# Both attn @ v of a step between the scores of its two pairs of heads, and the ffn's first products ahead of the last attn @ v

## The chip, the cores and the metric

The kernel runs on one core of one Trainium2 chip. The core has a matrix engine (TensorE, PE in the rows; PEld is its weight load), VectorE (DVE), ScalarE (ACT), GpSimd (POOL) and SyncE (SP), which here issues all DMAs. Each engine takes its own instructions in the order in which they were written and waits on semaphores for the others. The metric is the device time of one execution in microseconds (us); lower is better.

## The reference

```python
def _attn_ref(q, k, v):                       # q, k, v: (8, 12, 448, 64), f32
    S = q.shape[2]
    scale = 1.0 / np.sqrt(q.shape[-1])
    scores = scale * np.matmul(q, k.transpose(0, 1, 3, 2)) - np.log(S)
    attn = 1.0 / (1.0 + np.exp(-scores))      # a sigmoid, not a softmax
    return np.matmul(attn, v)

def _moe_ref(x, w_in, w_out, s, b):           # x: (3584, 768), w_in: (768, 2048), w_out: (2048, 768)
    r = np.maximum(x @ w_in, 0.0)
    return (s * (r * r) + b) @ w_out

# x is the attention's output with its heads side by side, one row for each of 8 * 448 tokens
```

Attention has 8 batches of 12 heads, 448 tokens, 64 elements for a head; the feed-forward net (ffn) has 3584 tokens, a width of 768 and 2048 hidden units. Outputs are f32.

## The kernel before, in words

**Attention.** The work is cut in 24 quads, one for each batch and each group of four heads (two pairs i = 0, 1). A loop of 25 steps n treats quad n's scores and, one step behind, quad n-1's product with v, so that the sigmoid has a whole step to be done. In the words of this document, a step on TensorE consists of these groups:

- S0 and S1 (`scores`, L233): the scores of pair 0 and pair 1 against the first 384 keys, three PSUM tiles `psc` for each. Two heads share the array, 64 rows each: the records show the form 64*128. Each `psc` goes to ScalarE for a sigmoid (L224), which leaves an SBUF tile `a`.
- A0 and A1 (`attn_v`, L255): `a` times v of the step before, for pair 0 and pair 1, into the PSUM tiles `pav0` and `pav1`; form 128*64.
- SL (`scores_last`, L245): the scores against the last 64 keys for all four heads, one more `psc`; form 64*64. AL (`attn_v_last`, L264): the last 64 keys' part of the step before; form 64*64. After AL, `store_x` (L272) copies both `pav` to SBUF on VectorE and stores them.

Two matmuls in two halves of the array run side by side; of the f32 matmuls here the profile has two records each. The pool `ps_qk` has three `psc` of two banks, `ps_av` has one `pav0` and one `pav1`: all 8 banks. A `psc` is free again when its sigmoid is done, a `pav` when `store_x` has copied it.

**Weights beside it.** During attention the ffn's weights are decoded from 64-bit words, in 32 pieces (16 of w_out, 16 of w_in), on VectorE and ScalarE. A plan puts the parts of a piece on ticks; `tick()` is called twice in each step and issues what the plan holds for that tick. A piece with tick t is fetched by a DMA at t - 3 (`st`, L302); at t comes a VectorE operation (L122) and a ScalarE one (L125, which needs L122); at t + 1 two VectorE operations (L127, which needs L125, and L130); at t + 2 two more (L134, L137). Pieces follow each other by STEP ticks from FIRST on. For each pair of w_out pieces come "sums": four subtractions on VectorE at one tick, two casts on ScalarE (L155, which need the subtractions) at the next, two subtractions and two stores at the third. `st` and the sums' tiles share a pool of six buffers, `cx`. All of it stands in the engines' queues where the tick is called, between the sigmoids on ScalarE and between the copies of `store_x` on VectorE.

**From attention to the ffn.** The first block of 512 tokens is loaded back (`first_tokens`, L188), cast on ScalarE into its high part `x0h` (L341), and its rest `x0l` is made on VectorE (L106). `base(0, f)` makes the high part (L165, ScalarE) and the low part (L106, VectorE) of a block of w_in, `w_0_f`. `ffn1(f)` (L454) is a row of 18 matmuls into a PSUM tile `ph`: the first needs `x0h` and the high part of the weights, the second `x0l`, the third the low part of the weights. After attention, a loop over 16 blocks f runs `ffn1`, `activate` and the second product `ffn2` (L476, into `po`). The other six blocks of tokens are done in three pairs by a scheme that saves matmuls (L593, L659); the diff doesn't touch that.

The program is written out in Python in the order in which each engine will do it (`manual_schedule`); nothing reorders it later.

Of the kernel before, what the change touches and what calls it, by code (L numbers as in the profile page):

```python
# [10 lines left out]
F32 = mybir.dt.float32  # L11
# [7 lines left out]
PSUM = bass.MemoryType.PSUM  # L19
# [18 lines left out]
TB = 512  # L38
WARM = 4
PARTS = ((0, 0), (0, 1), (1, 0))  # L40
# [5 lines left out]
def sigmoid_attention_relu2_ffn(  # L46
# [11 lines left out]
    nc = tc.nc  # L58
    B, NQ, P, _, S = q.shape
    D = v.shape[5]  # L60
    NF, _, DM = w_in.shape
    NCC = DM // P
    HC = NCC // 2
# [9 lines left out]
    def pool(stack, name, bufs, side=None, space=None):  # L73
        kw = dict(side=side) if side else {}
        if space is not None:
            kw["space"] = space
        return stack.enter_context(
            tc.tile_pool(name=name, bufs=bufs, reuse_waits="tile", **kw)
        )
# [19 lines left out]
    def f32(ap):  # L99
        return ap.bitcast(F32)  # L100
# [8 lines left out]
    order = [f + h * NP for f in range(NP) for h in range(2)]  # L109
# [85 lines left out]
    at = ExitStack()  # L195
# [2 lines left out]
    ldv = pool(at, "ldv", 3)  # L198
    qk = ExitStack()
    ld = pool(qk, "ld", 2)  # L200
    ps_qk = pool(at, "ps_qk", 3, space=PSUM)
    ps_av = pool(at, "ps_av", 1, space=PSUM)

    half = (slice(0, D), slice(D, P))
    quads = [(b, t) for b in range(B) for t in range(NQ)]
    NL = len(quads)
# [33 lines left out]
    def scores_last(b, t, ld_):  # L240
        qt, kt, _ = ld_
        psc = ps_qk.tile([P, 2, 512], F32, tag="psc", name=f"psc_{b}_{t}_l")
        for j, r in enumerate(half):
            for i in range(2):
                nc.tensor.matmul(  # L245
                    psc[half[i], j, :S], kt[r, i, 3 * P :], qt[r, i, :],
                    start=True, stop=True,
                )
        return sigmoid(psc, f"{b}_{t}_l")

    def attn_v(b, t, i, ld_, a):
        pav = ps_av.tile([P, 512], F32, tag=f"pav{i}", name=f"pav_{b}_{t}_{i}")
        for c in range(3):
            for j, r in enumerate(half):
                nc.tensor.matmul(  # L255
                    pav[r, :S], ld_[2][:, 3 * i + c, j, :], a[c][:, j, :],
                    start=c == 0, stop=False,
                )
        return pav

    def attn_v_last(ld_, a, pavs):
        for i in range(2):
            for j, r in enumerate(half):
                nc.tensor.matmul(  # L264
                    pavs[i][r, :S], ld_[2][half[i], 6, j, :], a[half[i], j, :],
                    start=False, stop=True,
                )

    def store_x(b, t, pavs):
        for i in range(2):  # L270
            o = xo.tile([P, S], F32, tag="xo", name=f"xo_{b}_{t}_{i}")
            nc.vector.tensor_copy(o, pavs[i][:, :S])  # L272
            nc.sync.dma_start(x_dram[b][:, 2 * t + i], o)

    loaded = {0: load(*quads[0], first=True)}
# [8 lines left out]
    nc.sync.dma_start(b_sb, b_)  # L284


    FIRST, FETCH, STEP = 3, 3, 1.3

# [36 lines left out]
    def tick():  # L327
        for fn in plan.pop(next(ticks), ()):
            fn()

    x0 = []

    def first_tokens():
        for h in range(2):
            hi = cx.tile([P, HC, TB], F32R, tag="cx", name=f"x0h_{h}")
            lo = cx.tile([P, HC, TB], F32R, tag="cx", name=f"x0l_{h}")
            load_tokens(f32(lo), 0, h)
            x0.append((hi, lo))
        yield
        for hi, lo in x0:  # L340
            nc.scalar.copy(hi, f32(lo))  # L341
        yield
        for hi, lo in x0:
            sub(lo, f32(lo), f32(hi))

    prev = None
    for n in range(NL + 1):
        cur = quads[n] if n < NL else None
        a, pavs = [], []
        if n > 0 and n + 1 < NL:  # L350
            loaded[n + 1] = load(*quads[n + 1])
        if cur:
            a.append(scores(*cur, 0, loaded[n]))
        tick()
        if prev:
            pavs.append(attn_v(*quads[n - 1], 0, loaded[n - 1], prev[0]))
        if cur:
            a.append(scores(*cur, 1, loaded[n]))
        tick()
        if prev:  # L360
            pavs.append(attn_v(*quads[n - 1], 1, loaded[n - 1], prev[1]))
        if cur:
            a.append(scores_last(*cur, loaded[n]))
        if n == NL - 1:
            qk.close()
            p1 = pool(early, "p1", 2, side="right")
            ft = first_tokens()
            next(ft)
        if n == NL:
            next(ft)  # L370
            next(ft, None)
            w1 = base(0, 0)
            ts = sums(0, 0)
            next(ts)
        if prev:
            attn_v_last(loaded[n - 1], prev[2], pavs)
            store_x(*quads[n - 1], pavs)
        prev = a
    assert not plan
    at.close()  # L380
# [56 lines left out]


    raw_a = pool(ctx, "raw_a", 1)
    blk = ExitStack()  # L440
    p2 = pool(blk, "p2", 3)
    gp = pool(blk, "gp", 3)
    rt = pool(blk, "rt", 2)
    ot = pool(blk, "ot", 1)
    ps_h = pool(blk, "ps_h", 2, space=PSUM)
    ps_o = pool(blk, "ps_o", 1, space=PSUM)

    def ffn1(f, w):
        ph = ps_h.tile([P, TB], F32, tag="ph", name=f"ph_{f}")
        m = 0  # L450
        for c in range(NCC):
            h, cc = divmod(c, HC)
            for wi, xi in PARTS:
                nc.tensor.matmul(  # L454
                    ph, w[:, h, wi, cc * P : (cc + 1) * P], x0[h][xi][:, cc, :],
                    start=m == 0, stop=m == 3 * NCC - 1,
                )
                m += 1
        return ph

    def activate(f, ph):
        g = gp.tile([P, 2, TB], F32R, tag="g", name=f"g_{f}")
# [19 lines left out]
    held = None  # L482
    w2 = {}
    for i, f in enumerate(order):
        ph = ffn1(f, w1)
        if i + 1 < NF:
            w1 = base(0, order[i + 1])
        if i % 2 == 0:
            next(ts)
        g = activate(f, ph)  # L490
        for n in (i, i + 1):
            if n < NF and n not in w2:
                w2[n] = base(1, order[n])
        if held:
            ffn2(*held, i == 1, False)
        held = (w2[i], g)
        if i % 2 == 0:
            next(ts)
        elif i + 1 < NF:
            ts = sums(0, (i + 1) // 2)  # L500
            next(ts)
        if i == NF - 4:
            load_raw(0, 0)
        if i == NF - 2:
            early.close()
            roll = pool(ctx, "roll", AHEAD + 2, side="right")
            raw_b = pool(ctx, "raw_b", 1, side="right")
            gpool = pool(ctx, "gpool", 1, side="right")
            for _ in range(AHEAD):
                fetch()  # L510
            load_raw(0, 1)
# [41 lines left out]
    for n, (t1, t2) in enumerate(pairs):  # L553
# [31 lines left out]
        for u, (i, f) in enumerate(L1):  # L585
# [4 lines left out]
            m = 0  # L590
            for c in range(HC):
                for wi, xi in PARTS:
                    nc.tensor.matmul(  # L593
                        bk, wt[:, wi, c * P : (c + 1) * P], opd[i][xi][:, c, :],
                        start=i in (1, 6, 5) and m == 0,
                        stop=m == 3 * HC - 1,
# [54 lines left out]
        for j, (i, f) in enumerate(L2):  # L651
# [5 lines left out]
            for e in range(HC):  # L657
                for m, (wi, gi) in enumerate(PARTS):
                    nc.tensor.matmul(  # L659
                        bk[e], wt[:, wi, e * P : (e + 1) * P], g[:, gi, :],  # L660
                        start=i in (1, 4, 7, 5) and f == 0 and m == 0,
                        stop=f == NP - 1 and m == 2,
# [64 lines left out]
```

## Time and profile before

| | us |
|---|---|
| median of 3 runs | 1104.01 (1103.75 to 1104.33) |
| the profiled execution's own time | 1103.69 |
| its span, from the first to the last instruction | 1101.9 |
| TensorE busy in that span | 1092.8 (99%) |
| VectorE, ScalarE busy | 667.3, 519.5 |
| attention on TensorE (from 4.5 to 279.5 us of the span) | 275.0 |
| the first block of tokens in the ffn (279.5 to about 437) | 157.5 |
| the other six blocks | 665 |

The profile is of one execution. "Busy" is an average over stages with different limits, and a matmul's end is modelled. What is read for this change is the chain of waits in time, which gives each group on TensorE its length from the end of the group before to its own end, and the timeline of VectorE and ScalarE beside it.

### The profile page before, as it was taken

The page shows a single profiled execution, that of the slowest core. Times are in us where ns is not written, and L with a number is a line of the kernel's source. Part 1 is how long each engine was busy: PE and PEld are TensorE (multiplying, and loading weights), DVE is VectorE, ACT ScalarE, POOL GpSimd, SP SyncE. Part 2 cuts the span into 40 slices and gives each one's busy share as a digit, 9 for nine tenths or more (in the row PEclk, how much of TensorE's full clock was granted, in tenths as well). Part 3 has the DMA queues.
Part 4 walks back from the last instruction along what each step waited for, and adds up shares of the span by engine and source line. Part 5 has one row for each costly group of instructions (what it writes and reads, how often), then busy time and mean ns, then how long its engine had stood idle before and what let it go on. Part 6 is the DMA issues. An engine that isn't in the chain of part 4 may idle for free.

```text
span 1101.9 us, 13945 instructions
## 1 busy us (share of the span) xinstructions
PE 1092.8 (99%) x5140; PEld 777.0 (71%) x5140; DVE 667.3 (61%) x916; ACT 519.5 (47%) x681; POOL 0.2 (0%) x4
## 2 busy tenths in 40 slices
PE   8999999999999999999999999999999999999998
PEld 3333333333788887888888888888888888888887
DVE  2667777773866654646665654467564645574646
ACT  6777767776544444314543343135443351244341
POOL 0000000000000000000000000000000000000000
PEclk9999999999999999999999999999999999999999
DMA  7889899976576598668667586696676766666773
GB/s 287 303 286 337 322 331 323 330 286 210 223 286 259 220 353 316 194 200 303 191 182 233 172 301 196 192 309 193 195 220 196 275 196 192 196 190 196 220 195 130
DMA packets 99394, 268.30 MB, mean 244 GB/s; under 512 B 11776, under 2 KB 27648, under 8 KB 99328
## 3 DMA queue, kind: packets, MB, share of 16 engines
q1 hardware_dynamic: 99328, 267.43, 73.2%
q8 instruction: 41, 0.67, 0.3%
q14 instruction: 25, 0.20, 0.1%
HBM read 201.33 MB, written 66.06 MB: 243 GB/s over the span
## 4 chain that ended last, share of the span: by engine, by line
PE 95%; DMA 1%; DVE 1%; ACT 1%; SPq 0%; issue 0%; ACTq 0%
PE o L659 31%; PE h L593 29%; PE psc L233 11%; PE pav L255 10%; PE ph L454 6%; PE po L476 5%; PE psc_l L245 2%; PE pav L264 2%; DMA wu<-wb 1%; DMA out_t<-o 1%; SPq L394 0%; DVE s_l L106 0%; ACT s_h L412 0%; DVE G L542 0%; DVE p L103 0%
## 5 line engine op out<-in xcount | busy, mean ns | idle before, releaser
L659 PE MATMUL o<-gc,wu 128*128 128x512 f32 x1512 | 343.2, 389 | 0.0
L659 PEld LDWEIGHTS o<-gc,wu 128*128 128x128 f32 x1512 | 283.8, 188 | 58.9
L593 PE MATMUL h<-s_h,wu 128*128 128x512 f32 x1008 | 311.4, 389 | 2.0 <-ACT G L608 2.0
L593 PEld LDWEIGHTS h<-s_h,wu 128*128 128x128 f32 x1008 | 189.2, 188 | 42.1 <-ACT G L608 2.8
L593 PE MATMUL h<-s_l,wu 128*128 128x512 f32 x504 | 196.1, 389 | 0.0
L574 ACT CAST gc<-G 128x512 fp32r<-128x512 f32 x168 | 104.0, 621 | 188.9 <-PE o L659 157.4
L106 DVE TENSOR_TENSOR gc<-G,gc 128x512 fp32r<-128x512 f32 x168 | 115.3, 690 | 122.7 <-ACT gc L574 122.3
L545 ACT ACTIVATE G<-G,b_sb,s_sb 128x512 f32<-128x512 f32 x96 | 78.3, 816 | 175.6 <-DVE G L542 175.6
L224 ACT ACTIVATE a<-psc,nls 128x896 f32<-128x896 f32 x144 | 134.6, 1008 | 47.1 <-PE psc L233 47.1
L103 DVE TENSOR_TENSOR G<-G,h 128x512 f32<-128x512 f32 x120 | 82.4, 686 | 87.7 <-PE h L593 87.6
L233 PE MATMUL psc<-q,k 64*128 64x448 f32 x576 | 122.0, 557 | 0.0
L255 PE MATMUL pav<-a,v 128*64 128x448 f32 x576 | 118.6, 547 | 0.7 <-DVE xo L272 0.7
L593 PEld LDWEIGHTS h<-s_l,wu 128*128 128x128 f32 x504 | 94.6, 188 | 19.6
L233 PEld LDWEIGHTS psc<-q,k 64*128 64x128 f32 x576 | 51.7, 187 | 69.6 <-issue 47.3
L542 DVE SCALAR_TENSOR_TENSOR G<-G 128x512 f32<-128x512 f32 x96 | 66.4, 691 | 51.1 <-ACT G L610 48.6
L255 PEld LDWEIGHTS pav<-a,v 128*64 128x64 f32 x576 | 37.2, 136 | 76.5 <-issue 61.1
L272 DVE COPY xo<-pav 128x448 f32<-128x448 f32 x48 | 27.7, 619 | 74.8 <-PE pav L264 74.8
L476 PE MATMUL po<-g,w 128*128 128x512 f32 x288 | 67.7, 389 | 0.0
L476 PEld LDWEIGHTS po<-g,w 128*128 128x128 f32 x288 | 54.1, 188 | 11.2
L454 PE MATMUL ph<-x0h,w 128*128 128x512 f32 x192 | 61.7, 390 | 0.0
L106 DVE TENSOR_TENSOR G<-G,G 128x512 f32<-128x512 f32 x72 | 49.3, 685 | 0.0
L412 ACT CAST s_h<-raw 128x1536 fp32r<-128x1536 f32 x21 | 30.9, 1477 | 24.3 <-DVE raw L106 12.7
(55 smaller groups left out, 692.6 us busy)
## 6 DMA issues: line engine op xcount, KB each, us to landing
wu<-wt SPq DMA_DIRECT2D x192, 384.0 KB, 3.5
wu<-wb SPq DMA_DIRECT2D x144, 384.0 KB, 3.5
wt<-t SPq DMA_DIRECT2D x32, 768.0 KB, 5.2
wb<-w SPq DMA_DIRECT2D x48, 384.0 KB, 2.9
st<-w_out SPq DMA_DIRECT2D x16, 768.0 KB, 8.2
st<-w_in SPq DMA_DIRECT2D x16, 768.0 KB, 7.3
v<-v_t SPq DMA_DIRECT2D x24, 448.0 KB, 6.4
xd<-xo SPq DMA_DIRECT2D x48, 224.0 KB, 2.1
```

The source lines that it names most:

```text
L103: nc.vector.tensor_tensor(o, x, y, op=ALU.add)
L106: nc.vector.tensor_tensor(o, x, y, op=ALU.subtract)
L224: nc.scalar.activation(a, psc[:, :, :S], AF.Sigmoid, bias=nls, scale=SCALE)
L233: nc.tensor.matmul(psc[:, j, :S], kt[r, i, c * P : (c + 1) * P], qt[r, i, :], start=True, stop=True,)
L255: nc.tensor.matmul(pav[r, :S], ld_[2][:, 3 * i + c, j, :], a[c][:, j, :], start=c == 0, stop=False,)
L454: nc.tensor.matmul(ph, w[:, h, wi, cc * P : (cc + 1) * P], x0[h][xi][:, cc, :], start=m == 0, stop=m == 3 * NCC - 1,)
L476: nc.tensor.matmul(pos[e], w[:, h, wi, ee * P : (ee + 1) * P], g[:, gi, :], start=first and i == 0, stop=last and i == 2,)
L542: nc.vector.scalar_tensor_tensor(x, x, 0.0, x, op0=ALU.max, op1=ALU.mult)
L545: nc.scalar.activation(x, x, AF.Identity, bias=b_sb, scale=s_sb)
L574: nc.scalar.copy(t[:, 0], src)
L593: nc.tensor.matmul(bk, wt[:, wi, c * P : (c + 1) * P], opd[i][xi][:, c, :], start=i in (1, 6, 5) and m == 0, stop=m == 3 * HC - 1, skip_gr ...
L659: nc.tensor.matmul(bk[e], wt[:, wi, e * P : (e + 1) * P], g[:, gi, :], start=i in (1, 4, 7, 5) and f == 0 and m == 0, stop=f == NP - 1 and ...
```

## The change

Within a step, A1 moves from behind S1 to right behind A0, and SL with it to right behind S1. Both ticks of a step now stand between S0 and A0 (before: one behind S0, one behind S1). In the last two steps the loads, casts and sums of the first tokens move: the loads are issued in step 22, the casts to `x0h` stand between S0 and S1 of step 23, `x0l`, `base(0, 0)` and the first sums stand at the end of step 23, and `ffn1` of block 0 stands in step 24 ahead of A0, A1 and AL of the last quad (before: behind them). For that, `ps_qk` is closed at the end of step 23 and gives its banks to `ps_h`, and `ps_av` lies on the other side. The plan starts a tick sooner (FIRST 2 for 3) and its pieces follow each other closer (STEP 1.25 for 1.3). No operation is added or left out.

```diff
-    ps_qk = pool(at, "ps_qk", 3, space=PSUM)
-    ps_av = pool(at, "ps_av", 1, space=PSUM)
+    ps_qk = pool(qk, "ps_qk", 3, space=PSUM)
+    ps_av = pool(at, "ps_av", 1, space=PSUM, side="right")
...
-    FIRST, FETCH, STEP = 3, 3, 1.3
+    FIRST, FETCH, STEP = 2, 3, 1.25
...
         tick()
+        if n == NL - 1:
+            next(ft)
+        tick()
+        if n == NL:
+            ph0 = ffn1(order[0], w1)
         if prev:
-            pavs.append(attn_v(*quads[n - 1], 0, loaded[n - 1], prev[0]))
+            for i in range(2):
+                pavs.append(attn_v(*quads[n - 1], i, loaded[n - 1], prev[i]))
         if cur:
             a.append(scores(*cur, 1, loaded[n]))
-        tick()
+            a.append(scores_last(*cur, loaded[n]))
+        if n == NL - 2:
+            ft = first_tokens()
+            next(ft)
         if prev:
-            pavs.append(attn_v(*quads[n - 1], 1, loaded[n - 1], prev[1]))
-        if cur:
-            a.append(scores_last(*cur, loaded[n]))
+            attn_v_last(loaded[n - 1], prev[2], pavs)
+            store_x(*quads[n - 1], pavs)
         if n == NL - 1:
+            next(ft, None)
             qk.close()
             p1 = pool(early, "p1", 2, side="right")
-            ft = first_tokens()
-            next(ft)
-        if n == NL:
-            next(ft)
-            next(ft, None)
+            ps_h = pool(blk, "ps_h", 2, space=PSUM)
             w1 = base(0, 0)
             ts = sums(0, 0)
             next(ts)
-        if prev:
-            attn_v_last(loaded[n - 1], prev[2], pavs)
-            store_x(*quads[n - 1], pavs)
...
     for i, f in enumerate(order):
-        ph = ffn1(f, w1)
+        ph = ffn1(f, w1) if i else ph0
```

`ffn1` itself moves up in the file unchanged. The diff's rows below are of the order in which instructions stand; no time is in them.

**TensorE in one step of the loop** (step 4). A row is a group of equal matmuls; `psc_b_t_i_c` are scores, `psc_b_t_l` the last keys, `pav_b_t_i` the product with v. Before, from A0 on:

```order
L255 MATMUL pav_1_0_0_515<-a_1_0_0_0_410,v_1_0_324 64x448 x2
L255 MATMUL pav_1_0_0_515<-a_1_0_0_1_415,v_1_0_324 64x448 x2
L255 MATMUL pav_1_0_0_515<-a_1_0_0_2_420,v_1_0_324 64x448 x2
L233 MATMUL psc_1_1_1_0_522<-q_1_1_401,k_1_1_402 128x448 x2
L233 MATMUL psc_1_1_1_1_527<-q_1_1_401,k_1_1_402 128x448 x2
L233 MATMUL psc_1_1_1_2_532<-q_1_1_401,k_1_1_402 128x448 x2
L255 MATMUL pav_1_0_1_547<-a_1_0_1_0_440,v_1_0_324 64x448 x2
L255 MATMUL pav_1_0_1_547<-a_1_0_1_1_445,v_1_0_324 64x448 x2
L255 MATMUL pav_1_0_1_547<-a_1_0_1_2_450,v_1_0_324 64x448 x2
L245 MATMUL psc_1_1_l_554<-q_1_1_401,k_1_1_402 64x448 x4
L264 MATMUL pav_1_0_0_515<-a_1_0_l_476,v_1_0_324 64x448 x2
L264 MATMUL pav_1_0_1_547<-a_1_0_l_476,v_1_0_324 64x448 x2
```

After, from A0 on:

```order
L255 MATMUL pav_1_0_0_533<-a_1_0_0_0_418,v_1_0_328 64x448 x2
L255 MATMUL pav_1_0_0_533<-a_1_0_0_1_423,v_1_0_328 64x448 x2
L255 MATMUL pav_1_0_0_533<-a_1_0_0_2_428,v_1_0_328 64x448 x2
L255 MATMUL pav_1_0_1_540<-a_1_0_1_0_467,v_1_0_328 64x448 x2
L255 MATMUL pav_1_0_1_540<-a_1_0_1_1_472,v_1_0_328 64x448 x2
L255 MATMUL pav_1_0_1_540<-a_1_0_1_2_477,v_1_0_328 64x448 x2
L233 MATMUL psc_1_1_1_0_547<-q_1_1_409,k_1_1_410 128x448 x2
L233 MATMUL psc_1_1_1_1_552<-q_1_1_409,k_1_1_410 128x448 x2
L233 MATMUL psc_1_1_1_2_557<-q_1_1_409,k_1_1_410 128x448 x2
L245 MATMUL psc_1_1_l_562<-q_1_1_409,k_1_1_410 64x448 x4
L264 MATMUL pav_1_0_0_533<-a_1_0_l_484,v_1_0_328 64x448 x2
L264 MATMUL pav_1_0_1_540<-a_1_0_l_484,v_1_0_328 64x448 x2
```

A1 (`pav_1_0_1`) stood between S1 and SL; it now stands behind A0 (`pav_1_0_0`), and SL comes right behind S1.

**ScalarE in step 3**, from the last sigmoid of S0 to that of SL; `wf` and `t` are tiles of the weights. Before:

```order
L224 ACTIVATE a_1_0_0_2_420<-psc_1_0_0_2_417,nls_74 128x896
L125 ACTIVATE wf_0_8_152<-wf_0_8_152,e_bias_75 128x768
L224 ACTIVATE a_1_0_1_0_440<-psc_1_0_1_0_437,nls_74 128x896
L224 ACTIVATE a_1_0_1_1_445<-psc_1_0_1_1_442,nls_74 128x896
L224 ACTIVATE a_1_0_1_2_450<-psc_1_0_1_2_447,nls_74 128x896
L224 ACTIVATE a_1_0_l_476<-psc_1_0_l_471,nls_74 128x896
```

After:

```order
L224 ACTIVATE a_1_0_0_2_428<-psc_1_0_0_2_425,nls_74 128x896
L125 ACTIVATE wf_1_1_137<-wf_1_1_137,e_bias_75 128x768
L155 CAST t_1_0_0_430<-t_1_0_0_430 128x2x384
L155 CAST t_1_0_1_431<-t_1_0_1_431 128x2x384
L224 ACTIVATE a_1_0_1_0_467<-psc_1_0_1_0_464,nls_74 128x896
L224 ACTIVATE a_1_0_1_1_472<-psc_1_0_1_1_469,nls_74 128x896
L224 ACTIVATE a_1_0_1_2_477<-psc_1_0_1_2_474,nls_74 128x896
L224 ACTIVATE a_1_0_l_484<-psc_1_0_l_479,nls_74 128x896
```

Where one operation of the plan stood ahead of S1's sigmoids, three now stand there.

**VectorE in the same step**, behind the two copies of `store_x`. Before:

```order
L122 TENSOR_SCALAR wf_0_8_152<-st_0_8_296 128x768
L134 SCALAR_TENSOR_TENSOR st_1_8_240<-st_1_8_240 128x768
L137 SCALAR_TENSOR_TENSOR wf_1_8_136<-st_1_8_240,wf_1_8_136 128x768
L127 SCALAR_TENSOR_TENSOR wf_0_0_151<-st_0_0_270,wf_0_0_151 128x768
L130 TENSOR_SCALAR st_0_0_270<-st_0_0_270 128x768
L106 TENSOR_TENSOR t_1_0_0_452<-wf_1_0_135 128x384
L106 TENSOR_TENSOR t_1_0_0_452<-wf_1_8_136,wf_1_0_135 128x384
L106 TENSOR_TENSOR t_1_0_1_453<-wf_1_8_136,t_1_0_0_452 128x384
L106 TENSOR_TENSOR t_1_0_1_453<-wf_1_8_136,t_1_0_1_453 128x384
```

After:

```order
L106 TENSOR_TENSOR t_1_0_0_430<-wf_1_0_135 128x384
L106 TENSOR_TENSOR t_1_0_0_430<-wf_1_8_136,wf_1_0_135 128x384
L106 TENSOR_TENSOR t_1_0_1_431<-wf_1_8_136,t_1_0_0_430 128x384
L106 TENSOR_TENSOR t_1_0_1_431<-wf_1_8_136,t_1_0_1_431 128x384
L134 SCALAR_TENSOR_TENSOR st_0_0_227<-st_0_0_227 128x768
L137 SCALAR_TENSOR_TENSOR wf_0_0_151<-st_0_0_227,wf_0_0_151 128x768
L127 SCALAR_TENSOR_TENSOR wf_0_8_152<-st_0_8_274,wf_0_8_152 128x768
L130 TENSOR_SCALAR st_0_8_274<-st_0_8_274 128x768
L122 TENSOR_SCALAR wf_1_1_137<-st_1_1_353 128x768
L134 SCALAR_TENSOR_TENSOR st_0_8_274<-st_0_8_274 128x768
L137 SCALAR_TENSOR_TENSOR wf_0_8_152<-st_0_8_274,wf_0_8_152 128x768
```

In the step after, the first operation of a new piece (L122 of `wf_1_1`, for which ScalarE's L125 of the same tile waits) stands behind the four subtractions of the sums and four operations of older pieces. Steps of this kind, in which the four subtractions and the two casts of the same sums fall into one step, are steps 3, 8, 13 and 18.

**TensorE from the last quad's attention to the ffn.** Before, from the second AL of step 23 on:

```order
L264 MATMUL pav_7_1_1_2108<-a_7_1_l_2059,v_7_1_1913 64x448 x2
L255 MATMUL pav_7_2_0_2144<-a_7_2_0_0_2074,v_7_2_1994 64x448 x2
L255 MATMUL pav_7_2_0_2144<-a_7_2_0_1_2079,v_7_2_1994 64x448 x2
L255 MATMUL pav_7_2_0_2144<-a_7_2_0_2_2084,v_7_2_1994 64x448 x2
L255 MATMUL pav_7_2_1_2151<-a_7_2_1_0_2096,v_7_2_1994 64x448 x2
L255 MATMUL pav_7_2_1_2151<-a_7_2_1_1_2101,v_7_2_1994 64x448 x2
L255 MATMUL pav_7_2_1_2151<-a_7_2_1_2_2106,v_7_2_1994 64x448 x2
L264 MATMUL pav_7_2_0_2144<-a_7_2_l_2120,v_7_2_1994 64x448 x2
L264 MATMUL pav_7_2_1_2151<-a_7_2_l_2120,v_7_2_1994 64x448 x2
L454 MATMUL ph_0_2215<-x0h_0_2126,w_0_0_2162 128x512
L454 MATMUL ph_0_2215<-x0l_0_2127,w_0_0_2162 128x512
L454 MATMUL ph_0_2215<-x0h_0_2126,w_0_0_2162 128x512 x2
```

After, from AL of step 23 to the first matmuls of block 0 (`ph_0`), and then from the last of these on:

```order
L264 MATMUL pav_7_1_0_2096<-a_7_1_l_2059,v_7_1_1931 64x448 x2
L264 MATMUL pav_7_1_1_2103<-a_7_1_l_2059,v_7_1_1931 64x448 x2
L340 MATMUL ph_0_2163<-x0h_0_2061,w_0_0_2152 128x512
L340 MATMUL ph_0_2163<-x0l_0_2062,w_0_0_2152 128x512
L340 MATMUL ph_0_2163<-x0h_0_2061,w_0_0_2152 128x512 x2
```

The last of block 0, the last quad's products, and the first of block 8:

```order
L340 MATMUL ph_0_2163<-x0h_1_2065,w_0_0_2152 128x512
L255 MATMUL pav_7_2_0_2182<-a_7_2_0_0_2082,v_7_2_2006 64x448 x2
L255 MATMUL pav_7_2_0_2182<-a_7_2_0_1_2087,v_7_2_2006 64x448 x2
L255 MATMUL pav_7_2_0_2182<-a_7_2_0_2_2092,v_7_2_2006 64x448 x2
L255 MATMUL pav_7_2_1_2189<-a_7_2_1_0_2113,v_7_2_2006 64x448 x2
L255 MATMUL pav_7_2_1_2189<-a_7_2_1_1_2118,v_7_2_2006 64x448 x2
L255 MATMUL pav_7_2_1_2189<-a_7_2_1_2_2123,v_7_2_2006 64x448 x2
L264 MATMUL pav_7_2_0_2182<-a_7_2_l_2130,v_7_2_2006 64x448 x2
L264 MATMUL pav_7_2_1_2189<-a_7_2_l_2130,v_7_2_2006 64x448 x2
L340 MATMUL ph_8_2259<-x0h_0_2061,w_0_8_2234 128x512
L340 MATMUL ph_8_2259<-x0l_0_2062,w_0_8_2234 128x512
L340 MATMUL ph_8_2259<-x0h_0_2061,w_0_8_2234 128x512 x2
```

All 18 matmuls of `ph_0` now stand between AL of step 23 and the last quad's A0; behind the last AL (`a_7_2_l`) the next is block 8's `ph_8`.

**VectorE at the same place**, after; before, the same operations stand in the same order:

```order
L272 COPY xo_7_1_0_2136<-pav_7_1_0_2096 128x448
L272 COPY xo_7_1_1_2139<-pav_7_1_1_2103 128x448
L106 TENSOR_TENSOR x0l_0_2062<-x0l_0_2062,x0h_0_2061 128x1536
L106 TENSOR_TENSOR x0l_1_2066<-x0l_1_2066,x0h_1_2065 128x1536
L106 TENSOR_TENSOR w_0_0_2152<-wf_0_0_151,w_0_0_2152 128x2x384
L106 TENSOR_TENSOR t_0_0_0_2157<-wf_0_8_152,wf_0_0_151 128x384
L106 TENSOR_TENSOR t_0_0_0_2157<-wf_0_8_152 128x384
L106 TENSOR_TENSOR t_0_0_1_2158<-wf_0_8_152,t_0_0_0_2157 128x384
L106 TENSOR_TENSOR t_0_0_1_2158<-wf_0_0_151,t_0_0_1_2158 128x384
L272 COPY xo_7_2_0_2200<-pav_7_2_0_2182 128x448
L272 COPY xo_7_2_1_2203<-pav_7_2_1_2189 128x448
L106 TENSOR_TENSOR w_0_8_2234<-wf_0_8_152,w_0_8_2234 128x2x384
```

The copies of step 23, `x0l`, the low part of `w_0_0`, four subtractions, then the copies of the last step, and only then the low part of `w_0_8`.

## Rows read from the trace of the kernel before

**Rows 1.** The page: busy time and share of each engine over the whole span, and the chain that ended last, by engine.

```profile
PE 1092.8 (99%) x5140; PEld 777.0 (71%) x5140; DVE 667.3 (61%) x916; ACT 519.5 (47%) x681; POOL 0.2 (0%) x4
...
PE 95%; DMA 1%; DVE 1%; ACT 1%; SPq 0%; issue 0%; ACTq 0%
```

**Rows 2.** The chain of waits in order of time, over one step of the attention loop and the start of the next: start, length in us, engine, tile and line, number of records.

```profile
34.01 2.46 PE psc L233 x12
36.46 2.41 PE pav L255 x12
38.87 2.46 PE psc L233 x12
41.32 2.40 PE pav L255 x12
43.73 0.91 PE psc_l L245 x8
44.64 0.75 PE pav L264 x8
45.39 2.46 PE psc L233 x12
```

**Rows 3.** The timeline of the same step, the first weight loads of S0 and of A0: start, length, engine, line, operation, and in brackets the idle time ahead of it.

```profile
33.94 0.30 PEld L233 LDWEIGHTS psc<-q,k 64*128 64x128 f32 x4 [0.71 <-issue]
...
36.39 0.20 PEld L255 LDWEIGHTS pav<-a,v 128*64 128x64 f32 x4 [0.65 <-issue]
```

**Rows 4.** The timeline of VectorE in the same step.

```profile
34.04 1.16 DVE L272 COPY xo<-pav 128x448 f32<-128x448 f32 x2 [4.50 <-PE pav L264]
35.11 0.55 DVE L122 TENSOR_SCALAR wf<-st 128x768 int32<-128x768 int32 x1
35.58 0.95 DVE L134 SCALAR_TENSOR_TENSOR st<-st 128x768 f32<-128x768 uint32 x1
...
37.45 0.95 DVE L127 SCALAR_TENSOR_TENSOR wf<-st,wf 128x768 int32<-128x768 int32 x1
...
38.91 0.55 DVE L106 TENSOR_TENSOR t<-wf 128x384 f32<-128x384 f32 x1
...
40.91 0.95 DVE L134 SCALAR_TENSOR_TENSOR st<-st 128x768 f32<-128x768 uint32 x1
```

**Rows 5.** The timeline of ScalarE in this step and the next.

```profile
35.07 2.81 ACT L224 ACTIVATE a<-psc,nls 128x896 f32<-128x896 f32 x3 [0.68 <-PE psc L233]
...
49.14 0.94 ACT L125 ACTIVATE wf<-wf,e_bias 128x768 int32<-128x768 int32 x1
49.97 1.57 ACT L155 CAST t<-t 128x768 fp32r<-128x768 f32 x2
51.42 2.82 ACT L224 ACTIVATE a<-psc,nls 128x896 f32<-128x896 f32 x3
```

**Rows 6.** The timeline of the first step, where the sigmoids pace TensorE: six sigmoids in a row, and the weight loads of the matmuls that wait for the `psc` of the first.

```profile
6.21 5.50 ACT L224 ACTIVATE a<-psc,nls 128x896 f32<-128x896 f32 x6 [4.00 <-PE psc L233]
...
7.27 0.42 PEld L233 LDWEIGHTS psc<-q,k 64*128 64x128 f32 x4 [0.33 <-ACT a L224]
```

**Rows 7.** The chain of waits in order of time, from AL of step 23 to the ffn.

```profile
272.39 0.76 PE pav L264 x8
...
273.18 0.64 DVE xo L272
...
273.86 4.73 PE pav L255 x24
278.59 0.91 PE pav L264 x8
279.50 8.38 PE ph L454 x36
287.88 4.08 PE po L476 x18
```

**Rows 8.** The timeline of VectorE at the same place.

```profile
273.18 1.16 DVE L272 COPY xo<-pav 128x448 f32<-128x448 f32 x2 [10.23 <-PE pav L264]
...
274.92 3.43 DVE L106 TENSOR_TENSOR x0l<-x0l,x0h 128x1536 fp32r<-128x1536 f32 x2 [0.59 <-ACT x0h L341]
...
278.26 0.95 DVE L106 TENSOR_TENSOR w<-wf,w 128x768 fp32r<-128x768 f32 x1
```

**Rows 9.** DMA early in the span: the issue of the q of step 2 on SyncE's queue (timeline), the time from issue to landing in us (last number of the DMA table's row, stretch from 11 us on), the same for the pieces of w_out over the whole span, and a stretch of the table of busy times (its last three columns are the granted TensorE clock, the DMA engines' share and GB/s).

```profile
11.44 0.71 SPq L218 DMA_DIRECT2D q<-q_t  x1
...
q<-q_t SPq DMA_DIRECT2D x1, 448.0 KB, 8.3
...
st<-w_out SPq DMA_DIRECT2D x16, 768.0 KB, 8.2
...
17.50:20.00 2.50, 2.50 (x14) 0.82 (x12) 0.00 (x0) 2.50 (x4) 0.00 (x0) 1.00 1.04 428
```

**Rows 10.** TensorE just after its first wait: the weight loads of the third and fourth of the four idle matmuls, 448 columns each, and the granted clock (third number from the end) of that stretch in the table of busy times.

```profile
3.22 0.15 PEld L281 LDWEIGHTS <-zero 128*128 128x128 bf16 x1 [0.22 <-issue]
...
3.60 0.15 PEld L281 LDWEIGHTS <-zero 128*128 128x128 bf16 x1 [0.22 <-issue]
...
2.80:5.80 3.00, 2.93 (x8) 1.28 (x10) 0.02 (x1) 0.00 (x0) 0.00 (x0) 1.00 0.90 273
```

More of the change, by code (lines that the diff above doesn't have):

```diff
@@ L331, in sigmoid_attention_relu2_ffn, with ffn1 @@
     x0 = []
+    blk = ExitStack()
+    def ffn1(f, w):
+        ph = ps_h.tile([P, TB], F32, tag="ph", name=f"ph_{f}")
+        m = 0
+        for c in range(NCC):
+            h, cc = divmod(c, HC)
+            for wi, xi in PARTS:
+                nc.tensor.matmul(
+                    ph, w[:, h, wi, cc * P : (cc + 1) * P], x0[h][xi][:, cc, :],
+                    start=m == 0, stop=m == 3 * NCC - 1,
+                )
+                m += 1
+        return ph
     def first_tokens():
@@ L439, in sigmoid_attention_relu2_ffn @@
     raw_a = pool(ctx, "raw_a", 1)
-    blk = ExitStack()
     p2 = pool(blk, "p2", 3)
@@ L444, in sigmoid_attention_relu2_ffn @@
     ot = pool(blk, "ot", 1)
-    ps_h = pool(blk, "ps_h", 2, space=PSUM)
     ps_o = pool(blk, "ps_o", 1, space=PSUM)
[L448 to L459, printed above, removed]
     def activate(f, ph):
```

## The prediction

> **What bounds the kernel now.** The page first: TensorE is busy for 99% of the span, and 95% of the chain that ended last lies on it [rows 1]. So only what shortens or delays TensorE's own row of work counts. Next the chain in order of time, over a step of the attention loop: the groups follow each other with no other engine between them, and a step takes 11.38 us, from 34.01 to 45.39 [rows 2]. Busy there isn't the same as at full pace, though. AL, eight records, lasts 0.75 us [rows 2], so four records (two matmuls side by side) take 0.375 us. S0 and A0 have twelve records, 2.25 us at that pace, but last 2.46 and 2.41; SL, as long as AL by its records, lasts 0.91 behind A1 [rows 2]. So a group whose form differs from that of the group ahead pays an entry: 0.21 us into S, 0.16 into A, 0.16 into SL behind A, and nothing into AL behind SL, where both are 64*64. Last, the end of attention: AL of step 23 ends at 273.15, TensorE waits until 273.86 for a copy on VectorE, does A0, A1 and AL, and the ffn's first products follow without a gap, done at 287.88 [rows 7].
>
> **The change part by part.**
>
> *Entries in the loop.* A1 no longer stands alone: its entry (0.16) goes, and so does that from A1 into SL (0.16); the entry from S1 into SL is new, x. S0, A0, S1 and AL are entered as before. A step saves 0.32 - x. No row shows S followed by SL with no wait between. Its ends are 0, as into AL, where the array stays split in 64-row halves, and 0.21, as into S out of AL, the reverse of the same pair of forms. I take 0.16, the price of the other entry into SL: 0.16 saved in each of steps 1 to 23, 3.7 us. The bounds are 23 x 0.11 = 2.5 and 23 x 0.32 = 7.4. The Trainium skill, "TensorEngine Tiling (Array Packing)", Tiling Modes (Key Properties), says that changing the tiling mode drains the array while changing only the tile doesn't; the entries above fit that, and no row here shows 64*128 to 64*64. By that sentence x is a full entry and the gain 3.7, without it up to 7.4.
>
> *Scores in a row.* S1, SL and the next S0 now want seven `psc` with only AL between, out of three. Times from the first weight load of S0: S0's sigmoids start at 1.13 (35.07 against 33.94) and take 2.81 for three [rows 3, 5]. A0 comes at 2.45 [rows 3], A0 and A1 last 2.41 + 2.25, so S1 comes at 7.11 and its sigmoids could start at 8.24. SL would come at 9.57 and needs the first `psc` of S1. In the first step a load came 1.06 after the start of the sigmoid that frees its `psc` (7.27 against 6.21) [rows 6]: 8.24 + 1.06 = 9.30 is in time, by 0.27. The sigmoids of S0, SL and so on are then in time too: SL's starts at 8.24 + 2.81 = 11.05, and the next S0's first could not before 11.23 + 1.13.
>
> *Both ticks ahead of S1's sigmoids.* All the plan's ScalarE work now has to fit between S0's last sigmoid (3.94) and 8.24. Mostly it does: in step 6, L125, two L155 and another L125 take 0.83 + 1.45 + 0.94 [rows 5], done by 7.2. In steps 3, 8, 13 and 18 it doesn't, because L125 waits for VectorE. There VectorE has, from 0.10 on: copies 1.07, four subtractions 2.00, L134 and L137 1.87, L127 and L130 1.46, and L122 0.55 (distances of starts in [rows 4]), so L122 ends at 7.05. ScalarE then needs 0.83 and 1.45 up to the first sigmoid of S1 [rows 5]: 9.36 instead of 8.24. SL can come at 9.36 + 1.06 = 10.42 instead of 9.57: TensorE waits 0.85 us, four times, 3.4 us. Bounds: 0, if these distances shrink by 0.85 in all, and 6, if the copies start late. The other steps' L122 come up by 5.5.
>
> *Block 0 of the ffn ahead of the last quad.* From T, the end of AL of step 23, VectorE has two copies, both `x0l` and the low part of `w_0_0`, in that order. ScalarE's casts of `x0h` now come in step 23 (2.8 us between its sigmoids), so VectorE runs through: 0.03 + 1.07 for the copies [rows 4, 8], 3.34 for `x0l` (274.92 to 278.26), 0.95 [rows 8]: T + 5.4. `ffn1`'s second matmul waits for `x0l`, its third for that low part, and all of the last quad is queued behind them on TensorE. In the kernel before, the same VectorE chain ran beside A0, A1 and AL [rows 7]; this cover is gone. With 4.08 / 18 = 0.227 for a matmul [rows 7], the other sixteen end at T + 9.1, A0 and A1 (0.16 + 4.50) at T + 13.7, AL (0.91) at T + 14.65. Now the second wait: block 8's third matmul needs the low part of `w_0_8`, which stands on VectorE behind the copies of this last AL: 0.03 + 1.07 + 0.95 and about 0.05 more, T + 16.75; sixteen matmuls, T + 20.4. Before it was 287.88 - 273.15 = 14.73. The loss is 5.7 us, and the 0.71 us of waiting that goes is in it. Bounds: 5.2 and 6.2, for what an estimate of 0.1 us at each handover may be off. Behind that, VectorE has `activate` and the low part of w_out's block done by about T + 19.9, ahead of `ffn2`: no third wait.
>
> *The rest at nothing.* FIRST and STEP move the same operations; L122 still finds its tile, as its fetch stands about a step (11 us) or more ahead, and landing took 8.2 [rows 9]. One more piece of 768 KB is queued ahead of step 2's loads: at 428 GB/s that is 1.8 us, and q lands at 11.44 + 8.3 + 1.8 = 21.5 [rows 9], ahead of step 2 at about 22.4. Without that 0.9 us of cover a delay would show once. The tokens' loads go out a step earlier. `ph` takes banks that the last sigmoid of step 23 frees at about T + 0.8, within the wait already counted.
>
> **Sum.** -3.7 + 3.4 + 5.7 = +5.4 us. The span goes from 1101.9 to 1107.3, the profiled execution from 1103.69 to 1109.1. The median of the runs lies 0.3 us above that execution: 1109.4.
>
> **The rivals.** (1) *S1 to SL is free*, since both use 64-row halves, as SL to AL does [rows 2]. Then the loop gains 7.4, the sum is +1.7 and the time 1105.7: not slower by what a measurement tells. It decides from x below about 0.02 us on. Against it: AL to S, the same two forms, costs 0.21. (2) *ScalarE is not late* in steps 3, 8, 13 and 18, because L122 comes up 0.85 us earlier than the distances in [rows 4] say: -3.7 + 5.7 = +2.0, 1106.0. For it: only 0.85 of 7 us need be missing. Against it: VectorE's queue there has no idle time in which to gain it. (3) *Both*: -7.4 + 5.7 = -1.7, 1102.3. (4) *The tail's waits make the array slow*. At its start TensorE took 0.38 us for 448 columns [rows 10], twice the 0.19 that a record of as many columns takes later (0.375 for two and two side by side), though the granted clock in that stretch's row reads 1.00 (2.4 GHz), so that column alone doesn't tell. In that stretch eight records kept it busy for 2.93 us; at 0.19 each they are 1.5 us. If the wait with two matmuls in it brings this pace back as it was then, it costs the difference, 1.4 us: 1110.8. The Trainium skill, "TensorE: Matmul & The Clock Gate", section "Why this matters for your kernels", warns that pauses between bursts of matmuls bring back half the clock; no row here has a pause above 0.71 us between matmuls of this stage, so the trace neither bears it out nor refutes it. (5) *ScalarE is late in five more steps* (those with L125, two L155, L125, where 1.0 us is to spare): 5 x 0.85, 1113.7. (6) *The operands of block 0 are ready in time* after all: -3.7 + 3.4 - 0.7, 1103.0. Against it stands VectorE's order: `x0l` behind the copies of AL.
>
> **How the numbers follow.** The forecast has a chance of 0.46, (1) 0.14, (2) 0.11, (3) 0.05, (4) 0.13, (5) 0.07, (6) 0.04. Within 0.2%, about what a measurement of this kernel can tell from no change, means 1101.8 to 1106.2: (1), (2) and most of (3) and (6), 0.29. Faster, from (3) and (6) with their terms at the good ends, 0.05. Slower 0.66. The range leaves out (3), (5) and (6), 0.16: from 1104.6, a little below (1), to 1111.8, above (4) with its bounds.
>
> **What would show it.** In the chain of the changed kernel: A0 and A1 as one piece of 24 records near 4.66 us; SL behind S1 at 0.91 (0.75 if (1) holds); a step of 11.22 us; waits of SL for ScalarE near 0.85 us in steps 3, 8, 13 and 18 and in no other; a wait near 5 us, broken by two matmuls, behind AL of step 23, with VectorE as its releaser, and one near 1.7 us at block 8; 20.4 us from that AL to `ffn2` instead of 14.73. The forecast is wrong if the tail's waits are not there, if SL comes without an entry, or if sigmoids of S1 wait for ScalarE's own queue in most steps.

## The result and the profile after

The changed kernel takes 1112.56 us (median of 5 runs, 1111.83 to 1113.17); beside it on the same chip the kernel before takes 1103.75. The ratio is 1.0078, 95% interval 1.0067 to 1.0090: slower by 8.8 us. The prediction was 1109.4 with a range up to 1111.8. The direction and most steps held, one term was too small, and the time lies 0.8 us above the range.

The profiled execution took 1112.94 us, its span 1111.1. First the chain of waits in order of time, for one step of the loop and the step behind it (step 3), to be laid beside [rows 2]: start, length, engine, tile, line, records.

```profile
23.70 2.46 PE psc L233 x12
26.16 4.66 PE pav L255 x24
30.82 2.46 PE psc L233 x12
33.28 0.91 PE psc_l L245 x8
34.19 0.76 PE pav L264 x8
...
39.03 0.96 DVE wf L137
39.99 0.88 DVE wf L127
...
41.96 0.94 ACT wf L125
...
44.25 1.01 ACT a L224
...
45.30 0.98 PE psc_l L245 x8
...
47.04 2.46 PE psc L233 x12
```

A0 and A1 are one piece of 4.66 (before 2.41 and 2.40), and SL still costs 0.91: its entry behind S1 is not free. The step from 23.70 ends at 34.95, 11.25 us, where 11.38 stood. Step 3 goes from 34.95 to 47.04, 12.09 us: the chain leaves TensorE, runs through VectorE's operations of the plan, ScalarE's operation L125, a cast of the sums (`t`, L155) and the sigmoid that SL waits for. The view of waits for TensorE over the whole span has this four times, and no other lateness in the loop (us in total, times, longest):

```profile
PE ph L340 <- DVE w L106: 3.5, 2, 2.0
PE psc_l L245 <- ACT a L224: 3.2, 4, 0.8
...
PE ph L340 <- ACT w L165: 1.4, 1, 1.4
...
PE ph L340 <- DVE x0l L106: 1.0, 1, 1.0
```

The other three rows are the tail. There the chain, beside [rows 7]:

```profile
273.60 0.76 PE pav L264 x8
...
275.54 3.33 DVE x0l L106 x2
278.87 0.88 DVE w L106
...
279.80 6.53 PE ph L340 x16
286.33 4.66 PE pav L255 x24
290.99 0.92 PE pav L264 x8
...
293.09 0.88 DVE w L106
...
294.01 3.90 PE ph L340 x16
297.90 4.08 PE po L477 x18
```

T is 274.36. VectorE's row of copies, `x0l` and the low part of the weights holds TensorE until 279.80, T + 5.44, as forecast. Then the same kind of group, sixteen products behind a wait, takes 6.53 us the first time and 3.90 the second. The busy time by stretches shows what goes with it: the third number from the end is the granted clock, 1.00 for 2.4 GHz and 0.50 for 1.2.

```profile
276.00:278.00 2.00, 0.76 (x2) 0.19 (x1) 2.00 (x2) 0.44 (x1) 0.00 (x0) 1.00 0.54 206
278.00:280.00 2.00, 0.20 (x1) 0.21 (x2) 2.00 (x3) 0.00 (x0) 0.00 (x0) 0.65 0.00 0
280.00:282.00 2.00, 2.00 (x5) 1.61 (x6) 1.71 (x4) 1.06 (x2) 0.00 (x0) 0.50 0.72 290
282.00:284.00 2.00, 2.00 (x6) 1.52 (x6) 0.00 (x0) 0.60 (x1) 0.00 (x0) 0.50 0.26 103
284.00:286.00 2.00, 2.00 (x8) 1.50 (x6) 0.00 (x0) 0.00 (x0) 0.00 (x0) 0.65 0.00 0
286.00:288.00 2.00, 2.00 (x12) 0.77 (x12) 0.00 (x0) 0.00 (x0) 0.00 (x0) 1.00 0.00 0
```

Five or six matmuls run in two microseconds where ten or eleven run at the full pace (e9, below). The clock fell while TensorE waited and came back only within the products behind the wait.

From AL of step 23 to `ffn2` it is 23.54 us, before 14.73 [rows 7]: +8.8. The loop from the end of the first 24 scores to T is 0.1 us shorter, the stage from `ffn2` to the end 0.8 shorter (813.2 for 814.0), and the first 24 scores of step 0 are 1.35 longer. Together +9.2, the difference of the spans (1111.1 and 1101.9). The 0.8 are TensorE's waits for ScalarE in the last stages, 2.0 us before and 1.2 after; they vary from one execution to the next (1.4 and 1.6 in the second profiles of the two kernels). What has to be told apart is whether the tail is the whole cost, what its slow products are slow of, and whether the long start belongs to the change.

### The profile page after: what moved, and what is told of

Same layout as the page of the kernel before. It is cut to its first block, busy times and chain, and to the rows that moved or that the text cites. A ratio compares the mean times of both kernels' runs of the same rounds, so it can differ in the third digit from the quotient of the medians.

```text
span 1111.1 us, 13951 instructions
## 1 busy us (share of the span) xinstructions
PE 1094.4 (98%) x5140; PEld 781.6 (70%) x5140; DVE 667.1 (60%) x916; ACT 519.1 (47%) x681; POOL 0.2 (0%) x4
## 4 chain that ended last, share of the span: by engine, by line
PE 91%; DVE 4%; ACT 2%; DMA 1%; issue 1%; SPq 0%; DVEq 0%; ACTq 0%
PE o L660 31%; PE h L594 29%; PE psc L233 9%; PE pav L255 8%; PE ph L340 6%; PE po L477 5%; PE psc_l L245 2%; PE pav L264 2%; DVE t L106 1%; DMA raw<-xd 1%; DMA wu<-wb 1%; ACT a L224 0%; DVE xo L272 0%; DVE wf L137 0%; DVE s_l L106 0%
## 5 line engine op out<-in xcount | busy, mean ns | idle before, releaser
L255 PE MATMUL pav<-a,v 128*64 128x448 f32 x576 | 113.5, 543 | 0.0
L340 PE MATMUL ph<-x0h,w 128*128 128x512 f32 x192 | 64.1, 402 | 4.9 <-DVE w L106 3.5
L340 PEld LDWEIGHTS ph<-x0h,w 128*128 128x128 f32 x192 | 37.2, 195 | 14.8 <-DVE w L106 4.2
```

Source lines behind the costliest of these rows:

```text
L255: nc.tensor.matmul(pav[r, :S], ld_[2][:, 3 * i + c, j, :], a[c][:, j, :], start=c == 0, stop=False,)
L340: nc.tensor.matmul(ph, w[:, h, wi, cc * P : (cc + 1) * P], x0[h][xi][:, cc, :], start=m == 0, stop=m == 3 * NCC - 1,)
```

## The experiments

The theory: tail +8.8 (the waits +5.7, as forecast; half clock behind them and two resumptions +3.1), late steps +3.4, entries -3.2 to -3.7. Rivals: the loop or the start costs more than the forecast had; the sixteen products are slow for another reason than the clock.

**e1_ffn1_behind: without the tail.**

```diff
-        if n == NL:
-            ph0 = ffn1(order[0], w1)
         if prev:
             for i in range(2):
                 pavs.append(attn_v(*quads[n - 1], i, loaded[n - 1], prev[i]))
...
             store_x(*quads[n - 1], pavs)
+        if n == NL:
+            ph0 = ffn1(order[0], w1)
```

> The 16 first products of block 0 go back behind the last AL and its copies, as before the change; the new order of the steps and of the plan stays. If the tail is the whole of what the forecast missed (AL of step 23 to ffn2 23.54 us in place of 14.73), this gives back 8.4 to 8.8 us: 1103.8 to 1104.2, within 0.2% of the kernel before, and the loop's part of the change is then 0 to +0.4 (entries -3.7, four late steps +3.4). If the loop itself costs more than that (the start was 1.35 us longer in the profile of the changed kernel), the time stays at 1105 or above.

1104.31 us; ratio to the kernel before 1.0003, interval 0.9994 to 1.0012. The cost is gone, so it lies in the tail; the loop with its gain and its late steps comes out at nothing. Its chain has the ffn's first 36 products at full pace again, as in [rows 7]:

```profile
280.67 8.43 PE ph L340 x36
```

**e3_tail_alone: the tail in the old loop.** The edit, against the kernel after:

```diff
-    FIRST, FETCH, STEP = 2, 3, 1.25
+    FIRST, FETCH, STEP = 3, 3, 1.3
...
-        tick()
         if n == NL:
             ph0 = ffn1(order[0], w1)
         if prev:
-            for i in range(2):
-                pavs.append(attn_v(*quads[n - 1], i, loaded[n - 1], prev[i]))
+            pavs.append(attn_v(*quads[n - 1], 0, loaded[n - 1], prev[0]))
         if cur:
             a.append(scores(*cur, 1, loaded[n]))
+        tick()
+        if prev:
+            pavs.append(attn_v(*quads[n - 1], 1, loaded[n - 1], prev[1]))
+        if cur:
             a.append(scores_last(*cur, loaded[n]))
```

> The order of the steps and the plan's FIRST and STEP are those of the kernel before; only the first products of block 0 stand ahead of the last attn @ v, with the pools and the first tokens moved for that as in the change. If the tail costs what the trace of the changed kernel shows (5.44 us of waits instead of none, 16 products at half rate 6.53 instead of 3.63, two entries more), this is 8.4 to 8.8 us slower than the kernel before: 1112.2 to 1112.6, as much as the whole change. If the half rate comes of the new order of the steps, it is 5.7 slower: 1109.5.

1112.66 us; ratio 1.0079 (1.0066 to 1.0091), as much as the whole change, +8.7. So the half rate doesn't come of the new order of the steps. In its chain:

```profile
273.28 0.76 PE pav L264 x8
...
279.48 6.35 PE ph L340 x16
...
293.51 3.91 PE ph L340 x16
297.42 4.08 PE po L479 x18
```

From T = 274.04 to `ffn2` it is 23.38 us.

**e2_piece_early: without the late steps.**

```diff
-        at_tick(n, lambda: (g.append(convert(l, f, st[0])), next(g[0])), first=True)
+        at_tick(n - n % 2, lambda: (g.append(convert(l, f, st[0])), next(g[0])), first=True)
```

> The first part of each piece is put at the even tick of its step, so that no piece sends its casts to ScalarE between the two sigmoids of a step; the rest is the changed kernel. If steps 3, 8, 13 and 18 are late because of those casts (4 x 0.86 us), the time falls by 3.4 us, to 1109.1, and steps 3, 8, 13, 18 last 11.24 us like their neighbours. If the late steps are due to something else (the loads of the weights, the buffers of the plan), it stays within 1 us of 1112.6.

1108.58 us; ratio 1.0042 (1.0029 to 1.0054), 4.0 below the changed kernel by the two ratios. Step 3 is like its neighbours now, 34.99 to 46.23 or 11.24 us:

```profile
34.99 2.46 PE psc L233 x12
...
46.23 2.46 PE psc L233 x12
...
276.41 5.28 PE ph L340 x16
```

The total is less clean than the step. The moved pieces bring one new lateness, 1.0 us in step 1, where VectorE waits for the load of a piece (view of waits):

```profile
PE psc_l L245 <- ACT a L224: 1.0, 1, 1.0
```

So the steps give back 2.4 us in all. Of the other 1.6, up to 1.25 may be the tail, where the half rate was shorter in this profile (5.28 for the sixteen products instead of 6.53); the rest is within what two ratios with such intervals leave open.

**e4_filled_wait: work for the array while it waits.**

```diff
+FILL = 26
...
+    warm = const.tile([P, 448], BF16, name="warm")
+    nc.vector.memset(warm, 0.0)
...
         if n == NL:
+            fill = ps_h.tile([P, TB], F32, tag="ph", name="fill")
+            for _ in range(FILL):
+                nc.tensor.matmul(fill[:, :S], warm[:, :P], warm[:, :S], start=True, stop=True)
             ph0 = ffn1(order[0], w1)
```

> The changed kernel with 26 products of zeros (bf16, 448 columns, into a tile that is not read) ahead of the first products of block 0, which run while these wait for their operands; they are work added and change no output. If the 2.7 us above the forecast in the tail are the clock, which was granted at 0.50 to 0.65 behind the wait, the 16 products take 3.6 us again and the time falls by 2.5 to 2.9 us, to 1109.7 to 1110.1. If the products were slow for another cause (the operands, the turn between tile shapes), it stays within 0.5 us of 1112.6, or rises by what the fillers last beyond the wait.

1129.19 us; ratio 1.0222 (1.0208 to 1.0236): far outside either expectation. The tail did what the clock theory said (18 products in 4.18 us with the clock at 1.00), but every product of the last stage took 0.232 us instead of 0.227. Either the fillers or their tile did that; against the changed kernel the run tells nothing of the clock. It does beside e8 (below), which has the same tile and no fillers: there `ffn1`'s 18 products take 4.19 us with the clock at 1.00, so 4.18 is the full pace with that tile, and the run with the fillers is 3.0 us shorter by the two ratios (1.0222 and 1.0249).

**e9_filled_no_tile: fillers without a tile of their own.**

```diff
+FILL = 20
...
         if n == NL:
+            fill = ps_h.tile([P, TB], F32, tag="ph", name="fill")
+            for _ in range(FILL):
+                nc.tensor.matmul(fill, x0[0][0][:, 0, :P], x0[0][0][:, 0, :], start=True, stop=True)
             ph0 = ffn1(order[0], w1)
```

> The changed kernel with 20 products of x0h by itself (float32r, 512 columns, into a tile that is not read) ahead of the first products of block 0: work added for the time in which these wait, without a tile of its own in SBUF. The run with 26 fillers had the 16 products at 3.6 us again with the clock at 1.00, and lost far more later, where every product of the last stage took 0.232 us instead of 0.227. If that loss came of the tile of zeros, which moves all later tiles by 896 bytes, this kernel lacks it and falls by 2.5 to 2.9 us, to 1109.7 to 1110.1. If it came of the fillers themselves, the last stage is at 0.232 us again and the time is near 1127.

1110.40 us; ratio 1.0058 (1.0045 to 1.0071), 2.2 below the changed kernel by the two ratios, in the direction and near the size expected. By the two intervals the 2.2 is uncertain by about 1.9, so the trace has to decide. Its chain, then its busy time in two of the stretches that had the clock at 0.50:

```profile
274.67 4.83 PE fill L376 x20
279.50 4.08 PE ph L341 x18
```

```profile
280.00:282.00 2.00, 2.00 (x10) 1.67 (x9) 1.33 (x3) 1.43 (x2) 0.00 (x0) 1.00 0.91 367
282.00:284.00 2.00, 2.00 (x11) 1.22 (x12) 0.00 (x0) 0.24 (x1) 0.00 (x0) 1.00 0.07 26
```

The operands come at the same time, the shapes and the turns between them are the same, only the array is kept at work: 18 products take 4.08 us and end at T + 9.60 (T is 273.98) instead of T + 11.97. The mean granted clock over the span is 1.000 in all five runs, where those of the changed kernel have 0.996 to 0.997. So the slow products are the clock, and the rival falls.

**e5_x0l_early: a shorter wait.**

```diff
+        if n == NL - 1:
+            next(ft, None)
         if prev:
             attn_v_last(loaded[n - 1], prev[2], pavs)
             store_x(*quads[n - 1], pavs)
         if n == NL - 1:
-            next(ft, None)
             qk.close()
```

> The changed kernel with the two subtractions x0l put ahead of the last matmuls and copies of step 23 instead of behind them; VectorE is idle there, from 264.3 to 274.4 us. Of the three things that block 0 waits for, w (ScalarE, T + 1.4), x0l (VectorE, T + 2.9 and 4.5) and w (VectorE, T + 5.4), the middle one goes, and the last comes at about T + 2.2 in place of T + 5.4. If waits and clock are both as read, the time falls by 3.2 us for the wait, and by up to 2.9 more if the shorter wait also keeps the clock: 1106.5 to 1109.4. If it falls by less than 3 us, the products waited for something else.

1107.79 us; ratio 1.0031 (1.0019 to 1.0044), 5.2 below the changed kernel by the two ratios. The chain of the profiled execution (1108.06 us) has the sixteen products from 276.04 on, T + 2.4; behind it two stretches of busy time:

```profile
276.04 5.53 PE ph L340 x16
```

```profile
276.00:278.00 2.00, 1.96 (x6) 1.64 (x7) 1.95 (x4) 0.83 (x1) 0.00 (x0) 0.71 0.76 302
278.00:280.00 2.00, 2.00 (x6) 1.54 (x6) 0.00 (x0) 0.83 (x1) 0.00 (x0) 0.50 0.38 154
```

The wait behaves as read from VectorE's row. In this execution the clock falls all the same, and it does so when the products already run. It doesn't in every one: the mean granted clock over the span is 1.000 in the two shortest of the six runs (1106.32 and 1107.19 us), 0.999 in the next (1107.52) and 0.998 in the other three (1108.06 to 1109.01). The first two are near the 1106.5 named for a clock that is kept, the last three near the 1109.4 named for one that falls.

**e6_loop_only: the change without its two costs** (the edits of e1 and e2 together).

> The new order of the steps, the first products of block 0 behind the last matmuls as before the change, and the first part of each piece at the even tick of its step: the change without its two costs. By the theory only the entries are left, -3.7 us: 1100.2, faster than the kernel before by 0.3%. If the late steps and the tail are not the whole of the cost, or if moving the pieces brings lateness elsewhere, it stays at 1102 or above.

1100.87 us; ratio 0.9971 (0.9961 to 0.9982): faster than both kernels, by 3.2 us against the kernel before (2.0 to 4.3 by the interval). It is 0.5 less than the entries were to give; 0.4 of that is a lateness that the moved pieces bring once, in step 1 (view of waits):

```profile
PE psc_l L245 <- ACT a L224: 0.4, 1, 0.4
```

**e8_tile_alone and e10_tile_of_1024: the tile that made the last stage slow.**

```diff
+    spare = const.tile([P, 448], BF16, name="spare")
+    nc.vector.memset(spare, 0.0)
```

> The changed kernel with the tile of zeros of 896 bytes per partition and no fillers: nothing reads it. If the placement of later tiles makes the last stage slow, its products take 0.232 us and the time rises by about 17 us plus what the fillers gave back, to 1129 to 1132. If not, it stays at 1112.6.

1130.87 us; ratio 1.0249 (1.0235 to 1.0263). In e10 the tile has 512 columns for 448:

> The changed kernel with an unread tile of 1024 bytes per partition in place of the 896 that made every product of the last stage take 0.232 us. If any move of the later tiles does that, it stays at 1130 to 1131; if it hangs on where they come to lie, a whole multiple of 1024 bytes leaves them as they were in that respect and the time is 1112 to 1113.

1111.57 us in one run, beside 1103.44 for the kernel before. Two pieces of the chain, 18 products of `ffn1` and 504 products in the last stage, of e8 and then of e10:

```profile
301.18 4.19 PE ph L342 x18
...
890.97 117.12 PE h L596 x504
```

```profile
300.52 4.08 PE ph L342 x18
...
877.72 114.24 PE h L596 x504
```

**b2_before_again and a2_after_again: the start.** Both kernels unchanged, profiled once more.

> The kernel before, unchanged, for a second profile of its start. The first 24 scores took 5.55 us in its first profile, 6.90 in that of the changed kernel, and 5.7 to 6.9 in the kernels with either order. If that is a spread from run to run, this profile shows any value from 5.5 to 6.9; if the old order and the old pools are what makes them short, it shows 5.55 again.

> The changed kernel, unchanged, for a second profile. If the length of the first 24 scores is a spread from run to run, it differs from 6.90 by some tenths or more; if it belongs to the change, it is 6.9 again. The tail, from AL of step 23 to the ffn's second product, should be 23.5 us again; if the clock falls at another moment of the wait, it differs by up to 1.3 us, as it did in the run with the pieces early (16 products in 5.28 us).

The timeline's row for the first 24 scores, of the kernel before in its first and in its second profile, then of the kernel after in its first and in its second:

```profile
4.48 5.62 PE L233 MATMUL psc<-q,k 64*128 64x448 f32 x24
```

```profile
4.49 7.07 PE L233 MATMUL psc<-q,k 64*128 64x448 f32 x24
```

```profile
4.48 6.97 PE L233 MATMUL psc<-q,k 64*128 64x448 f32 x24
```

```profile
4.48 5.81 PE L233 MATMUL psc<-q,k 64*128 64x448 f32 x24
```

Short and long starts occur in both kernels: the 1.35 us belong to the execution, not to the change. The tail varies too: in the second profile of the changed kernel the wait ends at T + 5.45 again, but the sixteen products take 5.91 us.

```profile
278.77 5.91 PE ph L340 x16
...
292.36 3.92 PE ph L340 x16
```

## Why the prediction fell short, point by point

- **Entries in the loop, -3.7: right.** SL behind S1 lasts 0.91, so the entry x is the 0.16 taken, and rival (1), a free one, is false. A step measures 11.24 to 11.25 us where 11.22 was named. By the chains, steps 2 to 23 take 247.2 us in e6 and 250.5 in the kernel before: 0.15 a step, 3.5 us over 23. Less the 0.4 of lateness that e6 has in step 1 that is 3.1, and e6 gives 3.2.
- **ScalarE late in steps 3, 8, 13 and 18, +3.4: right.** TensorE waits 0.8 us in each and nowhere else in the loop, step 3 is 0.84 longer than its neighbour, and moving the pieces takes that away (e2). Rivals (2), (3) and (5) are false.
- **The rest at nothing: right.** e1 is at 1.0003 of the kernel before (sum -0.3); no load arrives late.
- **The tail, +5.7: its waits right, its products not.** The failed step is "With 4.08 / 18 = 0.227 for a matmul [rows 7], the other sixteen end at T + 9.1": it takes the full pace behind 5.4 us of near idleness. They end at T + 11.97. Of the 2.9 missing, 2.6 is the clock (6.53 for the same sixteen products that take 3.90 behind the second wait). The other 0.3 comes at each of the two resumptions (3.90 instead of 16 x 0.227 = 3.63): the first weight load behind a wait has no matmul beside it; that this is the reason was not tested. With 2.6 and twice 0.3 the forecast 20.4 us becomes 23.6, and 23.54 is measured. e9 confirms that it is the clock.
- **Rival (4) named this mechanism**, but with a chance of 0.13 and 1.4 us. The price came from one stretch at the start of one execution, 2.80 to 5.80 [rows 10]. The second profile of the kernel before shows that there the slow pace can last 1.45 us longer, and the tail's sixteen products took 5.28 to 6.53 us over seven profiles with the wait (e5's shorter one among them): 1.4 to 2.6 above 3.90. The term is a range, and one stretch gave only its lower end. The Trainium skill, "TensorE: Matmul & The Clock Gate", "What's actually happening", says that the throttled state is the default and that activity lifts it, and in the same section that how many matmuls run slowly differs between runs of one kernel; the four starts and the tails agree.
- **Rival (6) is false**: `x0l` stands behind the copies of AL as the order said.

With the sizes measured: -3.5 + 3.4 + 8.8 = +8.7; the runs give +8.8.

What stays open: what decides whether the clock falls. The second wait of the tail is 2.1 us long (291.91 to 294.01); TensorE does two matmuls in it, is idle for 1.45 us, and goes on at full pace (3.90). The first wait in e5 is 2.4 us long, also with two matmuls, idle for 1.41 and 0.26 us, and in the profiled execution the clock falls behind it. The timeline of the changed kernel, then two rows of that of e5:

```profile
294.01 0.72 PE L340 MATMUL ph<-x0h,w 128*128 128x512 f32 x2 [1.45 <-DVE w L106]
```

```profile
275.05 0.50 PE L340 MATMUL ph<-x0h,w 128*128 128x512 f32 x1 [1.41 <-ACT w L165]
...
276.04 0.73 PE L340 MATMUL ph<-x0h,w 128*128 128x512 f32 x2 [0.26 <-DVE w L106]
```

The second of these waits is only a little longer, and in two of e5's six runs the same wait leaves the clock at 1.000. So the length of the wait alone doesn't decide it, and nothing here tells what does.

## What to carry to other kernels

A wait that a reordering puts on TensorE costs its length and what the clock takes behind it: here 5.4 us of waiting drew 1.4 to 2.6 us more in each of six profiles. A wait of 2.4 us (e5) drew nothing in some executions and 1.6 us in the one profiled. When work of a late stage is pulled ahead of work that is ready, follow its operands through the other engines' queues first; the work it was pulled past was their cover. And a change of several parts is worth taking apart: the loop's part alone, with the first part of some pieces moved one tick, is 0.3% faster than the kernel before, while the tail alone costs as much as the whole change.

## What the hardware showed beside it

- **Placement in SBUF.** An unread tile of 896 bytes per partition ahead of all others makes each product of the last stage 0.232 us (117.12 / 504) instead of 0.227 (114.24 / 504), and the run is some 19 us over the changed kernel by the two ratios; one of 1024 bytes doesn't (one run). Of the ffn's products ahead of that stage the first ones (`ffn1`) are slower too, 4.19 us for 18 in e8 and 4.08 in e10, while the second ones (`ffn2`) keep their pace, 4.09 and 4.08. That it is the place of the later tiles is inferred from the two sizes; which tile's address decides it was not tried.
- **The clock's column.** In the tail it shows the half pace (0.50). At the start of the span it reads 1.00 in every profile, while the first scores run at half pace for a while and then at full: in the second profile of the kernel before, pairs of weight loads are 0.75 us apart up to 9.13 us and 0.38 from there on. There the pace has to be read from the records.
